# The last expert's second layer of the last chunk in seven block products

## The chip, the cores and the metric

The kernel runs on one core of a Trainium2 chip. The metric is the time of one execution in microseconds (us) on the device; smaller is better. The core has TensorE (PE, matrix products, from SBUF into the accumulators of PSUM), VectorE (DVE), ScalarE (ACT) and GpSimd (POOL) for elementwise work, and SyncE (SP), which here issues DMAs. PE, DVE, ACT, POOL and SP each work through their own list of instructions in order and wait for each other by semaphores.

## The reference

An attention with pooled keys and values makes the tokens `x`; a layer of four experts follows, and its second product is what the change is about:

```
scores = scale * (q @ mean8(k).T);  x = softmax(scores) @ mean8(v)      # B=8, H=8, S=576, D=64
x -> (4608, 512);  p = domain_probs / sum(domain_probs)
for e in range(4):
    h = max(x @ w1[e], 0)             # (4608, 1024)
    out += p[:, e] * (h @ w2[e])      # (4608, 512)
```

## The kernel before

The 4608 tokens are worked on in nine chunks `c` of 512 tokens; the ninth (`c = 8`) holds the last 64 tokens of each of the eight batches (`x_rem`). For each chunk the four experts `e` follow each other. `order` lists the 32 pairs (c, e) from chunk 1 on, and a loop over slots `g` writes down, seven slots to a pair, which instruction each engine gets next. The schedule is by hand: every engine executes its instructions in the order in which this Python text calls them.

*Seven products.* Both layers cut their two matrices into 2 x 2 quarters and make the product from seven block products of sums and differences, not eight plain ones (Winograd's form). For the second layer, `quarters` names the quarters of the hidden matrix: `a11`, `a12`, `a21`, `a22` (rows are 256 tokens, columns 512 hidden values). `hidden_sums(c, e, part)` makes the sums on DVE by `combine` (L246), each over 128 x 1024 bf16:

- part 0: `S3 = a11 - a21`
- part 1: `S2 = a22 - S3`
- part 2: `a21 = a21 + a22`, in place
- part 3: `a12 = a12 - S2`, in place

`weight_sums` makes the sums of `w2` once, into `wt_bf[:, e]` (three quarters, `t[:, 0]` to `t[:, 2]`), and writes `b22 - b12` over the quarter `b12` of `w2_bf`. So after that the plain `b12` of an expert is gone.

*`down(c, e, step)`* (L746) is one of the seven block products: 8 matmuls of 128 x 256 outputs (L763), into one of two PSUM banks, `chains[0]` and `chains[1]` (o_ps in the profile). The steps of a pair lie in consecutive slots, between steps of the first layer (`up_product`, L695) of the next pairs. After each step, `add` (L842) multiplies the result by the token's probability and adds it to `acc` in SBUF: one DVE instruction for each block of 128 tokens, two to a step. For a step in `POOLED` (here step 4) the way is another: two ACT instructions write the scaled blocks to `addend` (L775), and one POOL instruction adds `addend` to `acc` (L777).

*`up_product`* (L695) works in `units[0]` and `units[1]`, two PSUM banks each (`unit` in the profile). Its step 5 ends with a relu on ACT that writes a half of `a21` (L716); its step 6 ends with a relu on DVE that writes a half of `a22` (L675). The last `up_product` of the kernel is unit 1, step 6, of the pair (8, 3), in the last slot, `g = 224`.

*The end.* In that slot step 6 of (8, 2) follows. Then `down_last` (L809) does the second layer of (8, 3) with eight plain block products: for each half `row` of the tokens and each half `col` of the columns, two blocks of 8 matmuls (L822) into one bank of `units` (for the last quarter into two banks), 64 matmuls. After each quarter come two `add`s on DVE and one `store` (L846). Since the plain `b12` of expert 3 is gone, `load_last_weights` (L798) has read it once more into `room`, by a DMA from POOL's queue in slot 210.

*`store`* for the last chunk issues two DMAs, one on SP's queue and one on ACT's (L856), each with the 64 tokens of one batch parity. The last quarter is stored block by block, so there are five stores, ten DMAs.

Of the kernel before, what the change touches and what calls it, by code (L numbers as in the profile page):

```python
# [9 lines left out]
ACT = mybir.ActivationFunctionType  # L10
ALU = mybir.AluOpType
# [6 lines left out]
def kernel(  # L18
# [10 lines left out]
    nc = tc.nc  # L29

    B, H, S, D = q.shape
    E, DM, F = moe_w1.shape
    P = nc.NUM_PARTITIONS
# [4 lines left out]
    NR = NT // P  # L38
    REM = S - NT
    KC = DM // P  # L40
    FCH = F // P
# [15 lines left out]
    HF, HN, HD, HK = FCH // 2, NT // 2, DM // 2, KC // 2  # L57
    FH = F // 2
    LO, HI = slice(0, HF), slice(HF, FCH)
    BLOCKS = 2  # L60
# [5 lines left out]
    units = [None, None]  # L66
    chains = [psum.tile([P, NT], F32, name=f"o_ps{i}") for i in range(2)]
# [6 lines left out]
    w2_bf = wpool.tile([P, E, FCH, DM], BF16, name="w2_bf")  # L74
    wu_bf = wpool.tile([P, E, 3, HK, FH], BF16, name="wu_bf")
    wt_bf = wpool.tile([P, E, 3, HF, HD], BF16, name="wt_bf")
    acc = const.tile([P, NR, DM], F32, name="acc")
    x_rem = const.tile([P, NPAIR, NT], BF16, name="x_rem")
    ident = const.tile([P, P], BF16, name="ident")
    partial = const.tile([P, 2, 2, NT], F32, name="partial")  # L80
    addend = const.tile([P, BLOCKS, HD], F32, name="addend")
    S2 = const.tile([P, HF, HN], BF16, name="S2")
    S3 = const.tile([P, HF, HN], BF16, name="S3")
# [90 lines left out]
    def load_q(b):  # L174
        q_sb = raws[("q", b)] = qpool.tile([P, H, NR, D], BF16, name="q_sb")
        src = q[b, :, 0:NT, :].rearrange("h (p r) d -> p h (r d)", r=NR)
        if b:
            nc.gpsimd.dma_start(out=q_sb[:].rearrange("p h r d -> p h (r d)"), in_=src)
            return
        for group, queue in enumerate((nc.sync, nc.scalar)):  # L180
            hs = slice(4 * group, 4 * group + 4)
            queue.dma_start(out=wide_q[:, hs], in_=src[:, hs])
# [38 lines left out]
    p_all = const.tile([P, NBLK, E], F32, name="p_all")  # L221
# [23 lines left out]
    def combine(dst, a, op, b):  # L245
        nc.vector.tensor_tensor(out=dst, in0=a, in1=b, op=op)  # L246
# [352 lines left out]
    hidden = {(0, 0): H_bufs[0], (0, 1): H_bufs[1], (0, 2): H_third, (0, 3): H_bufs[0]}  # L599
    order = [(c, e) for c in range(1, NCH) for e in range(E)]  # L600
# [130 lines left out]
    def quarters(c, e):  # L731
        H_sb = hidden[(c, e)]
        return H_sb[:, 0, 0], H_sb[:, 1, 0], H_sb[:, 0, 1], H_sb[:, 1, 1]

    def hidden_sums(c, e, part):
        a11, a12, a21, a22 = quarters(c, e)
        if part == 0:
            combine(S3[:], a11, ALU.subtract, a21)
        elif part == 1:
            combine(S2[:], a22, ALU.subtract, S3[:])  # L740
        elif part == 2:
            combine(a21, a21, ALU.add, a22)
        else:
            combine(a12, a12, ALU.subtract, S2[:])
# [48 lines left out]
        if fcs.stop == FCH:  # L793
            add(o_ps, c, e, r, slice(0, DM), True)

    room = wu_bf[:, 0, 0].rearrange("p k (i d) -> p (k i) d", d=HD)

    def load_last_weights():  # L798

        nc.gpsimd.dma_start(  # L800
            out=room, in_=moe_w2[E - 1][0:FH, HD:DM].rearrange("(fc p) d -> p fc d", p=P)
        )

    def last_weights(fc, col):
        if col and fc < HF:
            return room[:, fc, :]
        return w2_bf[:, E - 1, fc, col * HD:(col + 1) * HD]

    def down_last(c, e):  # L809

        H_sb = hidden[(c, e)]
        banks = units[0] + units[1]
        for row in (1, 0):
            for col in range(2):
                cols = slice(col * HD, (col + 1) * HD)
                both = [banks[2 * row + col]] * BLOCKS
                if not row and col:
                    both[1] = chains[0]
                ps = [ps[:, j * HD:(j + 1) * HD] for j, ps in enumerate(both)]
                for j in range(BLOCKS):  # L820
                    for fc in range(FCH):
                        nc.tensor.matmul(  # L822
                            ps[j], lhsT=H_sb[:, fc // HF, row, fc % HF, j * P:(j + 1) * P],
                            rhs=last_weights(fc, col),
                            start=(fc == 0 and (j == 0 or both[1] is not both[0])),
                            stop=(fc == FCH - 1), skip_group_check=True,
                        )
                for j in range(BLOCKS):
                    add(ps[j], c, e, row * BLOCKS + j, cols, False)
                    if not row and col:  # L830
                        store(c, row, cols, j)
                if row or not col:
                    store(c, row, cols)

    def add(o_ps, c, e, r, cols, first):

        prob = p_all[:, c * NR + r, e:e + 1]
        dst = acc[:, r, cols]
        if e == 0 and first:
            nc.scalar.activation(out=dst, in_=o_ps, func=ACT.Copy, scale=prob)  # L840
        else:
            nc.vector.scalar_tensor_tensor(  # L842
                out=dst, in0=o_ps, scalar=prob, in1=dst, op0=ALU.mult, op1=ALU.add,
            )

    def store(c, row, cols, j=None):  # L846
        rs = slice(row * BLOCKS, (row + 1) * BLOCKS)
        if j is not None:
            rs = slice(rs.start + j, rs.start + j + 1)
        if c < B:  # L850
            rows = out[c * S:c * S + NT, :].rearrange("(p r) d -> p r d", r=NR)
            nc.sync.dma_start(out=rows[:, rs, cols], in_=acc[:, rs, cols])
        else:
            by_batch = out.rearrange("(b s) d -> s b d", s=S)[NT:S]
            for bb, queue in enumerate((nc.sync, nc.scalar)):
                queue.dma_start(  # L856
                    out=by_batch[:, 2 * rs.start + bb:2 * rs.stop:2, cols],
                    in_=acc[bb * REM:(bb + 1) * REM, rs, cols],
                )
# [172 lines left out]
    with tc.manual_schedule(  # L1032
            engines={ENG.PE, ENG.DVE, ENG.Activation, ENG.Pool, ENG.SP}):
        load_q(0)
        load_first(k, "kraw", 0)
        load_first(k, "kraw", 1)
        choose_rows()
        make_identity(nc, ident[:])
        load_first(v, "vraw", 0)
        load_first(v, "vraw", 1)  # L1040
        nc.gpsimd.memset(p_all[:], 0.0)
        load_probs()
        load_w1(0)
        load_w1(1)
        clear()
        rows_chosen(0)
        rows_chosen(1)
        load_w1(2)
        load_w2(0)
        load_w1(3)  # L1050
        attention_first()
        psum_first.__exit__(None, None, None)
        psum_last = ctx.enter_context(
            tc.tile_pool(name="psum_last", bufs=1, space=bass.MemoryType.PSUM))
        units[:] = [[psum_last.tile([P, NT], F32, name=f"unit{u}{i}") for i in range(2)] for u in range(2)]
        load_whole(1, k, "kraw")
        load_q(1)
        load_w2(1)
        load_whole(1, v, "vraw", 2)
        load_w2(2)  # L1060
        first_chunk()


        N = len(order)
        later, amid = pieces_later()
        below_of = [(0, 3)] + order
        sums = {}
        for at, pieces in (((3,), weight_sums(3)[3:]), ((10, 10, 11, 11), weight_sums(1)), ((10, 15, 22, 14), weight_sums(2))):
            for slot, piece in zip(at, pieces, strict=True):
                sums.setdefault(slot, []).append(piece)  # L1070
        POOLED = (4,)
        for g in range(7 * N + 1):
            t, i = divmod(g, 7)
            if i in (0, 2, 3) and 1 < g < 7 * N:
                hidden_sums(*below_of[t], i)
            t2, i2 = divmod(g - 1, 7)
            ups = [(*order[t], 0, i)] if t < N else []
            if 0 <= t2 < N:
                ups.append((*order[t2], 1, i2))

            for args in reversed(ups) if g in amid else ups:
                up_product(*args)
            if g in amid:
                amid[g]()
            if i == 1 and 1 < g < 7 * N:
                hidden_sums(*below_of[t], i)
            if g == 0:

                down_plain(0, 2, NR - 1)
            else:  # L1090
                down(*below_of[t2], i2, t2 % 2, POOLED)
            for piece in later.get(g, ()):
                piece()
            for piece in sums.get(g, ()):
                piece()
            if g == 7 * (N - 2):
                load_last_weights()
        down_last(*order[-1])
# [1 line left out]
_INS = ['q', 'k', 'v', 'moe_domain_probs', 'moe_w1', 'moe_w2']  # L1100
_OUTS = [((4608, 512), 'float32')]
# [25 lines left out]
```

## Time and profile before

| what | value |
|---|---|
| median of 3 runs (lowest, highest) | 489.56 us (489.51, 490.53) |
| profiled execution, and its span from the first to the last instruction | 489.93 us, 488.2 us |
| PE busy, share of the span | 480.5 us, 98% |
| DVE busy | 376.9 us, 77% |
| ACT busy | 303.8 us, 62% |
| POOL busy | 119.4 us, 24% |
| `down_last`, 64 matmuls, first start to last end | 476.77 to 483.92 us |
| the ten DMA issues of the last chunk, first start to last end | 479.68 to 485.30 us |

All times in the text are counted from the start of the span. The profile is one execution, 0.37 us above the median. A busy PE is not a PE at its peak, since the records of matmuls overlap: one 128 x 256 matmul has a record of 0.27 us, while the next begins 0.109 us after it. In a line of the timeline stand the start, the duration, the engine, the line of the code, the operation with its output and inputs, and how many instructions were merged; in brackets, the idle time of the engine ahead of it and what ended that. "SPq" and "ACTq" are the issues of DMAs by these queues.

### The profile page before, as it was taken

How to read it: one execution, taken by the hardware profiler on the slowest of the kernel's cores; microseconds unless marked ns; L12 is line 12 of the kernel's file. 1: busy time of each engine (PE TensorE's matmuls, PEld its weight loads, DVE VectorE, ACT ScalarE, POOL GpSimd, SP SyncE). 2: the span in 40 equal slices, each digit the busy share in tenths (PEclk: the TensorE clock that was granted, in tenths of full speed). 3: DMA queues.
4: the chain of work that ended last, by engine and by line, in shares of the span. 5: the costliest groups of instructions: out<-in, count | busy, mean ns of one | idle time of the engine just before them, and what ended most of it. 6: DMA issues, size and time to landing. Idle time of an engine off the chain costs nothing.

```text
span 488.2 us, 11522 instructions
## 1 busy us (share of the span) xinstructions
PE 480.5 (98%) x4673; PEld 409.4 (84%) x4678; DVE 376.9 (77%) x758; ACT 303.8 (62%) x576; POOL 119.4 (24%) x120
## 2 busy tenths in 40 slices
PE   8999999999999999999999999999999999999996
PEld 4669568898888888888888888888898888888885
DVE  4779799989768976798679866997678766876674
ACT  5677446855676567656765567556755567556650
POOL 8520504242523154016321442111011101010000
PEclk9999999999999999999999999999999999999999
DMA  9999999994986489345954298311111010004003
GB/s 195 203 209 203 204 170 155 103 90 54 110 110 63 77 86 137 35 83 56 159 50 91 27 165 66 68 23 66 35 23 23 23 64 3 12 23 87 1 1 87
DMA packets 104996, 41.96 MB, mean 86 GB/s; under 512 B 75504, under 2 KB 104432, under 8 KB 104944
## 3 DMA queue, kind: packets, MB, share of 16 engines
q0 software_dynamic: 58496, 22.35, 41.8%
q1 hardware_dynamic: 45328, 17.84, 16.7%
q10 hardware_dynamic: 1120, 1.05, 0.6%
q8 instruction: 36, 0.59, 0.5%
q14 instruction: 16, 0.13, 0.1%
HBM read 45.69 MB, written 9.44 MB: 113 GB/s over the span
## 4 chain that ended last, share of the span: by engine, by line
PE 91%; DMA 3%; ACT 2%; DVE 2%; POOL 1%; issue 1%; POOLq 0%; ACTq 0%
PE unit L695 42%; PE o_ps L763 41%; DMA w_bf<-in_moe_w_dram 3%; PE att L467 1%; PE unit L822 1%; PE o_ps L617 1%; PE att L393 1%; ACT expT L549 1%; PE unit L617 1%; PE unit L393 0%; DVE wt_bf L246 0%; POOL wt_bf L142 0%; ACT qT L378 0%; DVE acc L842 0%; PE work_first L631 0%
## 5 line engine op out<-in xcount | busy, mean ns | idle before, releaser
L842 DVE SCALAR_TENSOR_TENSOR acc<-o_ps,p_all,acc 128x256 f32<-128x256 f32 (+1 forms) x285 | 126.9, 485 | 52.9 <-PE o_ps L763 36.5
L763 PEld LDWEIGHTS <-H 128*128 128x128 bf16 x1320 | 129.1, 98 | 15.5 <-issue 0.6
L695 PEld LDWEIGHTS <-w_bf 128*128 128x128 bf16 x1088 | 105.2, 98 | 13.0 <-issue 0.2
L675 DVE CUSTOM_DVE_ANT_0 H<-unit,partial 128x512 bf16<-128x512 f32 x128 | 87.2, 684 | 23.8 <-ACT partial L710 11.5
L763 PE MATMUL o_ps<-w_bf,H 128*128 128x256 bf16 x792 | 102.6, 273 | 0.4 <-ACT o_ps L771 0.4
L695 PE MATMUL unit<-xT,w_bf 128*128 128x256 bf16 x704 | 100.5, 273 | 0.0
L777 POOL TENSOR_TENSOR acc<-acc,addend 128x512 f32<-128x512 f32 x24 | 30.7, 1279 | 253.2 <-ACT addend L775 202.2
L710 ACT COPY partial<-unit 128x512 f32<-128x512 f32 x128 | 72.3, 592 | 30.2 <-PE unit L695 30.2
L695 PEld LDWEIGHTS <-wu_bf 128*128 128x128 bf16 x816 | 77.6, 98 | 11.7 <-issue 2.5
L695 PE MATMUL unit<-xs,wu_bf 128*128 128x256 bf16 x512 | 77.0, 273 | 0.0
L763 PE MATMUL o_ps<-wt_bf,H 128*128 128x256 bf16 x528 | 68.4, 273 | 0.0
L712 ACT ACTIVATE H<-unit 128x512 bf16<-128x512 f32 x66 | 39.8, 605 | 30.9 <-PE unit L695 30.9
L763 PEld LDWEIGHTS <-S 128*128 128x128 bf16 x528 | 51.7, 98 | 6.0
L716 ACT ACTIVATE H<-unit 128x512 bf16<-128x512 f32 x66 | 39.6, 602 | 25.6 <-PE unit L695 25.3
L708 ACT COPY unit<-unit 128x512 f32<-128x512 f32 x68 | 39.4, 582 | 23.6 <-PE unit L695 18.0
L695 PE MATMUL unit<-xs,w_bf 128*128 128x256 bf16 x256 | 38.4, 273 | 0.0
L840 ACT ACTIVATE acc<-o_ps,p_all 128x256 f32<-128x256 f32 x72 | 30.7, 485 | 9.4 <-PE o_ps L763 7.7
L152 POOL DMA_DIRECT2D kraw<-in_k_dram x20 | 26.3, 1317 | 39.0 <-DMA kraw<-in_k_dram 39.0
L695 PE MATMUL unit<-xT,wu_bf 128*128 128x256 bf16 x240 | 35.7, 272 | 0.0
L763 PE MATMUL o_ps<-w_bf,S 128*128 128x256 bf16 x264 | 34.2, 273 | 0.0
L763 PE MATMUL o_ps<-wt_bf,S 128*128 128x256 bf16 x264 | 34.2, 273 | 0.0
L152 POOL DMA_DIRECT2D vraw<-in_v_dram x20 | 28.4, 1420 | 18.8 <-DMA vraw<-in_v_dram 18.5
(162 smaller groups left out, 500.2 us busy)
## 6 DMA issues: line engine op xcount, KB each, us to landing
out_dram<-acc SPq DMA_DIRECT2D x32, 256.0 KB, 4.2
w_bf<-in_moe_w_dram POOLq DMA_DIRECT2D x10, 512.0 KB, 17.4
q_sb<-in_q_dram POOLq DMA_DIRECT2D x7, 512.0 KB, 9.6
vraw<-in_v_dram POOLq DMA_DIRECT2D x22, 144.0 KB, 6.5
kraw<-in_k_dram POOLq DMA_DIRECT2D x21, 144.0 KB, 5.7
w_bf<-in_moe_w_dram POOLq DMA_DIRECT2D x2, 1024.0 KB, 17.8
w_bf<-in_moe_w_dram POOLq DMA_DIRECT2D x4, 256.0 KB, 7.3
wt_bf<-in_k_dram POOLq DMA_DIRECT2D x4, 144.0 KB, 5.4
```

Of the source, the lines that this page charges most:

```text
L152: nc.gpsimd.dma_start(out=raw[:], in_=rows_of(src, b, 2 * part, 2 * part + 2), accum_op=ALU.add if part else ALU.bypass)
L617: nc.tensor.matmul(out_ps, lhsT=w1_bf[:, e, kc, fc * P:(fc + 1) * P], rhs=xT[:, kc, at], start=(kc == 0), stop=(kc == KC - 1), skip_group_ ...
L675: nc.vector._custom_dve(TENSOR_ADD_SAT, out=dst, in0=ps, in1=part, s0=LARGEST, s1=0.0)
L695: nc.tensor.matmul(ps[:, n * HN:(n + 1) * HN], lhsT=lhs[:, kc, f:f + P], rhs=rhs[:, kc, :], start=(not grows and n == 0 and kc == 0), stop ...
L708: nc.scalar.copy(out=banks[1][:], in_=ps)
L710: nc.scalar.copy(out=part[:, step - 2], in_=ps)
L712: nc.scalar.activation(out=quarter(0, 0), in_=ps, func=ACT.Relu)
L716: nc.scalar.activation(out=quarter(0, 1), in_=ps, func=ACT.Relu)
L763: nc.tensor.matmul(ps[:, j], lhsT=lhs[:, i, j * P:(j + 1) * P], rhs=rhs[:, i, :], start=(not grows and i == 0 and j == 0), stop=(i == HF - 1),
L777: nc.gpsimd.tensor_add(out=dst, in0=dst, in1=addend[:])
L840: nc.scalar.activation(out=dst, in_=o_ps, func=ACT.Copy, scale=prob)
L842: nc.vector.scalar_tensor_tensor(out=dst, in0=o_ps, scalar=prob, in1=dst, op0=ALU.mult, op1=ALU.add,)
```

## The change

`down_last` now makes the second layer of (8, 3) from seven block products, 56 matmuls. The sums grow in two banks for the token blocks, `X` (`units[0]`) and `Y` (`units[1]`), and in one bank for both blocks, `third` (the other of `chains`). The order on PE is: `a11` into X; then step 6 of (8, 2), which has been taken out of the slot loop and now goes the way of `POOLED` (ACT, then POOL); then `a21 + a22` into `third`, `S2` into X, `a12` into Y, `S3` into X, `less` into `third`, `a22` into X. Here `less` is `a12 - S2`, written to the quarter `a11` of the pair before. ACT copies the two blocks of X to Y after the first product. The first contents of `third` go by ACT to `spare` (a part of `partial`) and by POOL to `acc`; after each later product DVE has two adds. The five stores follow the adds: row 0 left, row 1 right, row 0 right, and row 1 left by blocks. The sums `S3` and, after it, `a21 + a22`, `S2` and `less` are new on DVE for this pair; `S3` is called ahead of the last `up_product`. `load_last_weights` is gone.

```diff
-    def load_last_weights():
...
-    def down_last(c, e):
...
+    def down_last(c, e, flip):
+
+        w, t = w2_bf[:, e], wt_bf[:, e]
+        a11, a12, a21, a22 = quarters(c, e)
+        less = hidden[(c, e - 1)][:, 0, 0]
+        X, Y = units
+        third = [chains[1 - flip][:, j * HD:(j + 1) * HD] for j in range(BLOCKS)]
...
+        def product(banks, lhs, rhs, grows):
+            for j in range(BLOCKS):
+                for i in range(HF):
+                    nc.tensor.matmul(
+                        banks[j][:, 0:HD], lhsT=lhs[:, i, j * P:(j + 1) * P], rhs=rhs[:, i, :],
+                        start=(not grows and i == 0 and (j == 0 or banks is not third)),
+                        stop=(i == HF - 1), skip_group_check=True,
+                    )
+
+        def add_both(banks, row, cols, room=None, stored=True, split=False):
+            if room is not None:
                 for j in range(BLOCKS):
...
+                    prob = p_all[:, c * NR + row * BLOCKS + j, e:e + 1]
+                    nc.scalar.activation(out=room[:, j], in_=banks[j][:, 0:HD], func=ACT.Copy, scale=prob)
+                dst = acc[:, row * BLOCKS:(row + 1) * BLOCKS, cols]
+                nc.gpsimd.tensor_add(out=dst, in0=dst, in1=room)
+            else:
                 for j in range(BLOCKS):
...
+                    add(banks[j][:, 0:HD], c, e, row * BLOCKS + j, cols, False)
+                    if split:
                         store(c, row, cols, j)
...
+            if stored and not split:
+                store(c, row, cols)
+
+        product(X, a11, w[:, LO, left], False)
+        for j in range(BLOCKS):
+            nc.scalar.copy(out=Y[j][:, 0:HD], in_=X[j][:, 0:HD])
+        hidden_sums(c, e, 2)
+        hidden_sums(c, e, 1)
+        combine(less, a12, ALU.subtract, S2[:])
+        down(c, e - 1, 6, flip, (6,))
+        product(third, a21, t[:, 0], False)
+        add_both(third, 1, right, spare, stored=False)
+        product(X, S2, t[:, 1], True)
+        add_both(X, 0, right, stored=False)
+        product(Y, a12, w[:, HI, left], True)
+        add_both(Y, 0, left)
+        product(X, S3, w[:, LO, right], True)
+        add_both(X, 1, right)
+        product(third, less, w[:, HI, right], True)
+        add_both(third, 0, right)
+        product(X, a22, t[:, 2], True)
+        add_both(X, 1, left, split=True)
...
+            if g == 7 * N:
+                hidden_sums(*order[-1], 0)
...
-            else:
+            elif g < 7 * N:
                 down(*below_of[t2], i2, t2 % 2, POOLED)
...
-            if g == 7 * (N - 2):
-                load_last_weights()
-        down_last(*order[-1])
+        down_last(*order[-1], (N - 1) % 2)
```

More of the change, by code (lines that the diff above doesn't have):

```diff
@@ L794, in down_plain @@
             add(o_ps, c, e, r, slice(0, DM), True)
-    room = wu_bf[:, 0, 0].rearrange("p k (i d) -> p (k i) d", d=HD)
-    def load_last_weights():
[L800 to L807, printed above, removed]
-    def down_last(c, e):
[L811 to L819, printed above, removed]
-                for j in range(BLOCKS):
[L821 to L827, printed above, removed]
@@ new lines, in down_last @@
+    def down_last(c, e, flip):
[4 more added lines that the diff above has]
+        third = [chains[1 - flip][:, j * HD:(j + 1) * HD] for j in range(BLOCKS)]
+        left, right = slice(0, HD), slice(HD, DM)
+        spare = partial[:].rearrange("p u a t -> p (u a t)")[:, 0:BLOCKS * HD].rearrange(
+            "p (j d) -> p j d", j=BLOCKS)
+        def product(banks, lhs, rhs, grows):
[8 more added lines that the diff above has]
+            if room is not None:
+                for j in range(BLOCKS):
+                    prob = p_all[:, c * NR + row * BLOCKS + j, e:e + 1]
[3 more added lines that the diff above has]
+            else:
@@ L828, in down_last @@
                 for j in range(BLOCKS):
-                    add(ps[j], c, e, row * BLOCKS + j, cols, False)
-                    if not row and col:
+                    add(banks[j][:, 0:HD], c, e, row * BLOCKS + j, cols, False)
+                    if split:
                         store(c, row, cols, j)
-                if row or not col:
-                    store(c, row, cols)
+            if stored and not split:
+                store(c, row, cols)
+        product(X, a11, w[:, LO, left], False)
```

## The prediction

> **What bounds the kernel now.** I read the page first, for its chain of work that ended last:
>
> ```profile
> PE 91%; DMA 3%; ACT 2%; DVE 2%; POOL 1%; issue 1%; POOLq 0%; ACTq 0%
> ```
>
> TensorE (PE) carries nine tenths of the way to the end, so work taken from it can shorten the run, but only in the few microseconds that the change touches. So I read the same chain in order of time, for the last part (start, duration, what, how many):
>
> ```profile
> 476.06 0.87 PE o_ps L763 x8
> 476.93 6.11 PE unit L822 x56
> 483.05 0.89 PE o_ps L822 x8
> 483.93 0.02 issue
> 483.96 0.48 DVE acc L842
> ```
>
> The 64 matmuls of `down_last` (L822) stand end to end: 6.98 us from 476.93 to 483.92, 0.109 us each. Nothing makes PE wait; then comes one add of VectorE (DVE). Next the timeline before them (start, duration, engine, line, operation), for what PE, DVE, ScalarE (ACT) and GpSimd (POOL) do when the last hidden values arrive:
>
> ```profile
> 474.79 0.60 ACT L716 ACTIVATE H<-unit 128x512 bf16<-128x512 f32 x1
> 475.46 0.60 PE L695 MATMUL unit<-xs,w_bf 128*128 128x256 bf16 x4
> 475.66 0.88 DVE L842 SCALAR_TENSOR_TENSOR acc<-o_ps,p_all,acc 128x256 f32<-128x256 f32 x2 [0.62 <-PE o_ps L763]
> 475.90 1.04 PE L763 MATMUL o_ps<-wt_bf,H 128*128 128x256 bf16 x8
> 476.45 0.68 DVE L675 CUSTOM_DVE_ANT_0 H<-unit,partial 128x512 bf16<-128x512 f32 x1
> ```
>
> The plain products multiply what ACT and DVE wrote, with nothing between. Seven products need sums of those values, and the relu at 476.45, the last of them, ends at 477.13. Last, the stores, from narrow windows of the timeline:
>
> ```profile
> 483.12 0.60 SPq L856 DMA_DIRECT2D out_dram<-acc  x1
> 483.12 0.63 ACTq L856 DMA_DIRECT2D out_dram<-acc  x1
> 483.79 0.86 ACTq L856 DMA_DIRECT2D out_dram<-acc  x1
> 484.47 0.54 SPq L856 DMA_DIRECT2D out_dram<-acc  x1
> 484.75 0.55 ACTq L856 DMA_DIRECT2D out_dram<-acc  x1
> ```
>
> The last add ends at 484.44, but ACT's queue is still issuing the store before, so its half of the last store goes out at 484.75. The span ends 3.48 us after that (landing, then the closing steps). So three issues in a row on one queue already set the end: the third-last store counts as much as the last.
>
> **What goes off the path at no cost.** The reload of 512 KB (L800) issues at 439.5 in 0.84 us of POOL's queue and lands 5.9 us later, 30 us before its reader; POOL is 24% busy. Removing it gives nothing.
>
> **PE.** Eight matmuls fewer: 8 x 0.109 = 0.87 us less. The first of the seven products takes the slots from 475.90 (its `a11` is long written, its banks were emptied at 475.04); step 6 of expert 2 moves behind it, 476.77 to 477.64. The next product reads `a21` after the sum `a21+a22`. On DVE that sum is queued so: the two adds at 475.66, the new sum `S3` in the slot of 476.45, the relu 0.60 later at 477.05, ending at 477.73, then `a21+a22`, which waits for the relu's result. What a wait between two DVE operations costs is in these rows:
>
> ```profile
> 464.23 0.68 DVE L246 TENSOR_TENSOR S<-H 128x1024 bf16<-128x1024 bf16 x1
> 464.83 0.68 DVE L675 CUSTOM_DVE_ANT_0 H<-unit,partial 128x512 bf16<-128x512 f32 x1
> ...
> 23.57 0.69 DVE L246 TENSOR_TENSOR S<-H 128x1024 bf16<-128x1024 bf16 x1
> 24.36 0.69 DVE L246 TENSOR_TENSOR S<-H,S 128x1024 bf16<-128x1024 bf16 x1
> ```
>
> Independent, the second starts 0.60 after the first, before the first has ended; dependent, 0.10 after its end. So `a21+a22` runs 477.83 to 478.51. The Trainium skill (VectorE: DVE Perf Modes, The DRAIN you can't avoid) says that a semaphore after each operation costs nothing extra; by that rule the sum would start 0.19 earlier and my total be +0.8. These rows show 0.79 against 0.60, and I go by them.
>
> PE's weight load starts 0.05 after such a result (13.82 to 13.87 at L455), so at 478.56. Whether the load's own 98 ns then adds is not shown (bounds 0 and 0.10; I take 0.10, since here nothing covers it). PE restarts at 478.66 instead of 477.64: a stall of 1.02 us, at least 0.92. It eats the 0.87 saved: the last matmul ends near 484.06, 0.14 later than 483.92.
>
> Later sums do not stop PE: `S2` ends at 479.11 and is read at 479.53; `S4` (into `less`) ends at 479.89 and is read at 482.15.
>
> **The adds.** From 478.66 the products take 0.87 us each: `third` 478.66, X 479.53, Y 480.41, X 481.28, `third` 482.15, X 483.03 to 483.90. Each is followed by two DVE adds, 0.40 apart back to back and 0.48 to the end: 0.80 against 0.87, so DVE keeps up. With 0.04 from a matmul's end to an add, and block ends 0.60 and 1.04 after a product's start, the adds start at 480.17 and 480.61, 481.05 and 481.49, 482.03 and 482.43, 483.23 and 483.63, 484.03 and 484.42. Each X product finds its bank read 0.4 us or more before. `third` is one bank for both blocks, so its adds wait for the whole product (483.19), and the last two adds queue behind them: the last ends at 484.90, 0.46 later than now.
>
> **ACT and POOL.** New: two copies X to Y, four scaled copies, two POOL adds. The pair of scaled copies at 473.97 (L775) took 0.84, POOL's add behind it (L777) 1.27, starting 0.13 after the pair's end. The second copy must wait for the relu (477.73), the scaled pair of step 6 ends near 478.97, its POOL add at 480.37; the pair of `third` ends at 480.57, its POOL add at 481.97. The add on row 1, right half, waits for it: 482.03 instead of 481.92, swallowed with 0.4 to spare. Cost nothing; uncovered from 0.4 late on.
>
> **The stores.** They leave at 482.0, 482.9, 484.14 (`third`), 484.54 and 484.93, against 479.68, 481.47, 483.12, 483.79 and 484.47 now. On ACT's queue from 484.14: 0.63, gap 0.04, 0.86, gap 0.10, and the last issue starts at 485.77, where it starts at 484.75 now: +1.02. If the 0.86 was a chance and the issue takes the 0.55 of its neighbour: +0.71. SP's (0.6 and 0.56) stays ahead of ACT's.
>
> Sum: +1.0 us. Bounds: +0.6 with both low ends, +1.2 if the relu behind `S3` takes 0.79 too where I took 0.60. The profiled execution of 489.93 (span 488.2, 1.7 around it) becomes 490.9; it was 0.37 above the median of 489.56, so the median becomes 490.6. A measurement of this kernel can tell about 0.2%, here 0.98 us: the sum lies on that edge.
>
> **Rivals.**
> - *The stores come too close* (18%). All of them now start after 482.0. In the window from 484.0 to 486.6 this trace moves 0.52 MB at a mean of 202 GB/s. If 1.05 MB ran at that rate from 483.2 (1.2 us after the first issue), the last byte would go at 488.4 instead of 486.5: +1.9, 491.5. Against it: slices of that window reach 300 GB/s, which would need 3.5 us and hide behind the issues. The Trainium skill (DMA: Bandwidth & Descriptors, Issuing engines are not separate DMA queues) says that DMAs of both queues run on the same 16 engines and interleave; that speaks for this rival.
> - *The issues get shorter* (14%). The end is the queue of issues; with 0.55 each after `third`, the last starts 0.5 to 0.7 later than now: 490.1 to 490.3, not slower by what can be told. It decides if ACT's issue of the fourth store takes under 0.8. For it: nine of ten issues take 0.54 to 0.73. Against: it is the same place in the same sequence.
> - *Adds fall behind PE* (9%). If the POOL adds or the scaled copies are over 0.4 late, the adds of row 1 hold the X bank and PE waits again: each 0.5 late is 0.5 at the end, +1.5 to +2, up to 491.6. POOL's 24 adds at 1.26 to 1.58 speak against it.
> - *Faster by over 0.2%* (4%). Even without any stall, `third` would be stored at 483.2, no earlier than the third-last store now, so the queue of issues would give back the 0.87. It would take the stall gone and shorter issues both. The sum would have to be ready at 477.59, and DVE's last adds before it cannot start before 475.66.
>
> **The numbers.** The sum as worked has 55%; its own range is +0.8 to +1.2, and 32 of the 55 fall above 0.98, since small waits that I did not price only add. Slower: 32 + 18 + 9 = 59%; same: 23 + 14 = 37%; faster 4%. The range goes from just under the shorter issues, 489.9, to the adds' 491.6.
>
> **What would show it.** PE should idle 0.9 to 1.0 us ahead of the first `third` product, released by DVE's L246, and nowhere else after it; its last matmul should end near 484.0. The adds should end near 484.9, and the third-last store should issue near 484.1. A PE gap ahead of an X product would mean the adds' rival; a longer way from the last issue to its landing, the stores'. A span under 488.2 would prove the order of steps wrong.

## The result and the profile after

The changed kernel takes 490.97 us (median of 9 runs, 490.77 to 492.64), the kernel before 489.89 us (median of 9, 489.44 to 490.53). The ratio is 1.0028, with a 95% interval of 1.0018 to 1.0038. The forecast was +1.0 us; the medians differ by 1.08 us, the ratio says 0.9 to 1.9 (its middle is 1.4).

The profiled execution has a span of 489.0 us, only 0.8 above the one before. But it came to the end of the common part 0.30 us sooner. That point lies anywhere from 474.8 to 477.0 us in the profiles of this case, so these 0.30 us of one pair of profiles say nothing about the change. So from here on times are also counted from A, the start of the last first-layer product's matmuls (475.46 before, 475.16 after). From A to the end of the span it is 12.77 us before and 13.87 after: +1.10, in line with the medians.

The chain that ended last, in order of time (start, duration, what, how many), of the changed kernel:

```profile
475.34 0.02 issue
475.36 0.88 DVE acc L858 x2
476.24 0.60 DVE S L246
476.84 0.60 DVE H L675
477.44 0.61 DVE H L246
478.05 0.05 issue
478.09 1.05 PE o_ps L810 x8
479.14 2.62 PE unit L810 x24
481.76 0.89 PE o_ps L810 x8
482.65 0.02 issue
482.67 1.27 DVE acc L858 x3
```

Before, the matmuls of `down_last` stood in this chain end to end. Now the chain leaves PE at 475.34, runs through five DVE operations in a row (two adds, `S3`, the relu and `a21 + a22`), and comes back to PE at 478.09. PE's own list was free at 477.34, so it stood 0.75 us. After that its six products follow each other without a gap, 0.87 us each, and the chain ends in DVE's adds. The last matmul ends 8.35 us after A, where it ended 8.46 after A before: 0.87 saved, 0.75 given back.

The stores of the changed kernel, from narrow windows of the timeline (start, duration, queue):

```profile
481.44 0.74 ACTq L872 DMA_DIRECT2D out_dram<-acc  x1
482.71 0.63 ACTq L872 DMA_DIRECT2D out_dram<-acc  x1
483.58 0.71 ACTq L872 DMA_DIRECT2D out_dram<-acc  x1
484.33 0.80 ACTq L872 DMA_DIRECT2D out_dram<-acc  x1
485.23 0.55 ACTq L872 DMA_DIRECT2D out_dram<-acc  x1
```

The last issue starts 10.06 after A (9.29 before), and the last DMA lands 12.29 after A (11.47 before). So the end loses 0.82 us by the landing, although PE was done 0.11 sooner. What is left of the 1.10, 0.29 us, comes after the landing, in the closing steps (below).

What the DMA engines moved shows the rest. The row of GB/s in 40 slices of 0.25 us, from 3 us after A on, of the kernel before:

```profile
GB/s 0 0 0 0 0 0 0 0 0 0 147 188 160 344 201 41 0 168 184 201 344 152 0 66 209 156 271 348 312 303 250 176 8 0 0 0 0 0 0 0
```

and of the changed kernel:

```profile
GB/s 0 0 0 0 0 0 0 0 0 0 0 0 0 0 0 0 0 0 102 201 152 279 311 143 234 246 271 340 266 213 311 307 275 308 254 17 0 0 0 0
```

Before, there are pauses between the stores. After, 1.05 MB leave in one piece, from 7.5 to 11.9 us after A, some 240 GB/s.

### The profile page after: what moved, and what is told of

The parts are those of the page before. It is cut to its first block, busy times and chain, and to the rows that moved or that the text cites. A ratio compares the mean times of both kernels' runs of the same rounds, so it can differ in the third digit from the quotient of the medians.

```text
span 489.0 us, 11529 instructions
## 1 busy us (share of the span) xinstructions
PE 480.2 (98%) x4670; PEld 408.6 (84%) x4670; DVE 378.9 (77%) x762; ACT 305.9 (63%) x582; POOL 121.6 (25%) x121
## 3 DMA queue, kind: packets, MB, share of 16 engines
q10 hardware_dynamic: 1120, 1.05, 0.6%
## 4 chain that ended last, share of the span: by engine, by line
PE 91%; DMA 3%; DVE 3%; ACT 1%; POOL 1%; issue 1%; DVEq 0%; POOLq 0%; ACTq 0%
PE unit L695 42%; PE o_ps L763 41%; DMA w_bf<-in_moe_w_dram 3%; PE att L467 1%; PE o_ps L617 1%; PE att L393 1%; DVE acc L858 1%; PE unit L617 1%; PE unit L810 1%; PE unit L393 0%; DVE wt_bf L246 0%; POOL wt_bf L142 0%; PE o_ps L810 0%; ACT qT L378 0%; PE work_first L631 0%
## 5 line engine op out<-in xcount | busy, mean ns | idle before, releaser
L777 POOL TENSOR_TENSOR acc<-acc,addend 128x512 f32<-128x512 f32 x25 | 32.5, 1300 | 256.3 <-ACT addend L775 204.6
```

Of the source, the lines that this page charges most:

```text
L777: nc.gpsimd.tensor_add(out=dst, in0=dst, in1=addend[:])
```

## The experiments

All times after A, in us; the ratio is to the kernel before, with its 95% interval.

| kernel | ratio | PE ends | last add ends | last issue | last landing | end |
|---|---|---|---|---|---|---|
| before | 1 | 8.46 | 8.98 | 9.29 | 11.47 | 12.77 |
| changed | 1.0028 (1.0018 to 1.0038) | 8.35 | 9.17 | 10.06 | 12.29 | 13.87 |
| e1 no sums | 1.0011 (1.0002 to 1.0021) | 7.59 | 8.41 | 9.29 | 11.56 | 13.14 |
| e2 one last store | 1.0017 (1.0008 to 1.0026) | 8.35 | 9.17 | 9.20 | 12.20 | 13.59 |
| e3 before, one last store | 0.9993 (0.9983 to 1.0003) | 8.46 | 8.98 | 9.02 | 11.81 | 12.86 |
| e4 sum ahead | 1.0034 (1.0021 to 1.0046) | 8.38 | 9.26 | 10.16 | 12.46 | 14.05 |
| e5 step 6 on DVE | 1.0030 (1.0018 to 1.0042) | 8.35 | 9.17 | 10.04 | 12.44 | 13.73 |
| e6 before, 5 memsets | 1.0004 (0.9995 to 1.0013) | 8.46 | 8.98 | 9.29 | 11.47 | 12.77 |
| e7 without block 0 | 1.0013 (1.0004 to 1.0023) | 8.35 | 9.17 | 9.20 | 11.89 | 13.26 |
| e8 other order | 1.0029 (1.0019 to 1.0039) | 8.81 | 9.63 | 10.50 | 12.89 | 14.49 |
| e9 before, 6 memsets | 1.0001 (0.9991 to 1.0012) | 8.46 | 8.98 | 9.29 | 11.46 | 13.08 |
| e10 half a store | 1.0026 (1.0017 to 1.0036) | 8.35 | 9.17 | 10.07 | 12.06 | 13.64 |
| e11 one store more | 1.0037 (1.0024 to 1.0051) | 8.35 | 9.17 | 10.93 | 12.98 | 14.45 |

The intervals are 0.1% wide to either side, 0.5 us. The traces tell smaller things, though each is one execution: the kernel before, e6 and e9, which differ only by memsets long before the end, agree within 0.01 us up to the landing.

**e1: the sums taken out.**

```diff
-        hidden_sums(c, e, 2)
-        hidden_sums(c, e, 1)
-        combine(less, a12, ALU.subtract, S2[:])
...
-            if g == 7 * N:
-                hidden_sums(*order[-1], 0)
```

> Leaves out the four sums of the last pair (S3, a21 + a22, S2, less), so the products of the end read what lies there; all else is as in the changed kernel. Theory (PE stands 0.75 us for VectorE's queue ahead of the first product into third): the gap ahead of it goes, and the end comes 0.7 to 0.8 us earlier than in the changed kernel, some 0.3 above the kernel before, because the queue of store issues gives back the rest. Rival (the adds and the stores alone set the end, the PE gap is covered): under 0.2 us earlier than the changed kernel. Rival (GpSimd's chain decides): the add on row 1, right half, still starts at the end of GpSimd's second add, and less than 0.4 us is won.

PE's gap is gone (it ends at 7.59, 0.87 before the kernel before) and the landing is 0.73 earlier, as the theory said. But with the whole saving on PE the last issue is at 9.29, the very place of the kernel before, and the landing at 11.56 is 0.09 behind it. The third-last store is where they meet: it goes out at 7.66 in both, because in both PE has done the same 56 matmuls behind the first layer when its result is complete. The eight that are saved would have come behind it. In the changed kernel the stall of 0.75 lies ahead of it and moves it to 8.42. So the stall is what separates the changed kernel's landing from the one before; and with these five stores the 0.87 saved on PE does not reach the end, stall or not.

**e2, e7, e10, e11: what sets the end behind the adds.**

```diff
-        add_both(X, 1, left, split=True)
+        add_both(X, 1, left)
```

> The changed kernel with its last quarter stored as one pair of DMAs in place of two pairs. Theory (three issues in a row on ScalarE's queue set the end): the last issue starts near 484.4 in place of 485.2; its DMA is twice as large, which gives back 0.2 to 0.4; the end comes 0.4 to 0.7 us earlier. Rival (the transfers bind): the last landing stays where it is, within 0.2 us.

The last issue came 0.86 earlier, the landing 0.09, the end 0.28 (the rest lies in the closing steps). The theory's 0.4 to 0.7 failed; the rival's 0.2 at the landing held. The larger DMA alone does not explain it: in e3 one of that size lands 2.8 us after its issue, here 3.0.

```diff
-                    if split:
+                    if split and j:
                         store(c, row, cols, j)
```

> The changed kernel without the fourth store (the first block of the last quarter is left out of the output). Theory (the issues in a row set the end): the last issue starts near 484.36 in place of 485.2 and lands 2.2 us later, 0.8 us earlier than in the changed kernel. Rival (the transfers bind): the last landing moves by what 128 KB take at 300 GB/s, 0.4 us, or less.

The issue again 0.86 earlier, the landing 0.40, as the rival had it. Against e2, with the last issue at the same place (9.20), 128 KB less land 0.30 earlier: the transfers.

```diff
-        add_both(third, 0, right)
+        add_both(third, 0, right, stored=False)
+        store(c, 0, slice(HD, HD + HD // 2))
```

> The changed kernel with the third-last store (row 0, right) writing half of its columns; the other half is left out of the output. As many issues, 128 KB less. Theory of the prediction (issues in a row set the end): the last issue near 10.06 us and the last landing near 12.29 us after the start of the last first-layer product, as in the changed kernel, within 0.1. Rival, which the runs with one issue less now speak for (the transfers of all five stores run without a break and set the end): the last landing is 0.3 to 0.4 earlier although the last issue stays.

With all issues in place (the last at 10.07) and 128 KB less, the landing is 0.23 earlier. A queue of issues alone would have left it where it was; transfers alone would have given 0.3 to 0.4, if their time goes by bytes; the number of DMA packets (1185) stayed. The last landing comes 1.99 after its issue here, 2.23 in the changed kernel.

```diff
-        add_both(third, 0, right)
+        add_both(third, 0, right, split=True)
```

> The changed kernel with the third-last store cut into two, one for each block: one pair of issues more, the same bytes, and half of them 0.4 us earlier. Theory of the prediction: the last issue on ScalarE's queue is 0.3 to 0.5 later, and the last landing as much later. Rival (the transfers set the end): the last landing stays within 0.15 of the changed kernel's or comes earlier, as long as the last issue is less than 0.5 later.

One pair of issues more, the same bytes: the last issue was 0.87 later, not 0.3 to 0.5, and the landing 0.69 later. The slices of this run, from 3 us after A, show the DMA engines running dry:

```profile
GB/s 0 0 0 0 0 0 0 0 0 0 0 0 0 0 0 0 0 0 106 201 156 283 283 180 225 238 254 283 340 258 262 230 144 0 188 242 148 193 17 0
```

So both limits are there, and in the changed kernel they lie within some 0.3 us of each other. With fewer issues the bytes bind (e2, e7); with fewer bytes the landing comes 0.23 us earlier and then, it seems, the issues bind (e10); with more issues the issues bind (e11). The Trainium skill (DMA: Bandwidth & Descriptors, Issuing engines are not separate DMA queues) has one half of this: DMAs that several engines issue run on the same 16 DMA engines. The same section of the Trainium skill calls the time of an issue usually small beside the DMA. It is not small here: 0.55 to 0.80 us for each issue of the changed kernel on ACT's queue, against 2.2 from the last issue to its landing, and five issues on that queue.

**e3: the last store in one on the kernel before.**

```diff
-                    if not row and col:
-                        store(c, row, cols, j)
-                if row or not col:
-                    store(c, row, cols)
+                store(c, row, cols)
```

> The kernel before with its last quarter computed in one go and stored as one pair of DMAs; the quarter then lies in one bank, so both adds wait for its last matmul. Theory: the last add ends 0.4 later, the last issue starts near 484.9 in place of 484.75, and the larger DMA adds 0.2 to 0.4: 0.3 to 0.6 us slower than the kernel before. If the split did nothing there: within 0.2 us.

The expectation misdescribed the edit: the last quarter still lay in two banks, so the first block's add was not held up, and the last issue came at 9.02, not later. The landing is 0.34 later, because the DMA twice as large took 2.8 us from its issue in place of 2.2. The time is the same within the interval. So splitting the last store gains a third of a microsecond at the landing there, and 0.25 of it is lost in the closing steps: from landing to end it is 1.04 in e3 and 1.29 before. With one pair of stores less they are shorter in e2 and e7 too (1.40 and 1.37 in place of 1.58), but in e11, with one pair more, they also are (1.46). What they depend on is not shown.

**e4: the sum that PE waits for called ahead of the relu.**

```diff
                 hidden_sums(*order[-1], 0)
+                hidden_sums(*order[-1], 2)
...
-        hidden_sums(c, e, 2)
         hidden_sums(c, e, 1)
```

> The changed kernel with a21 + a22 called ahead of the last relu. Theory: the gap ahead of the first product into third falls from 0.75 to some 0.15 us and one of 0.3 opens ahead of the next, for S2; but the relu is 0.6 later, so is ScalarE's copy to Y, and behind it the scaled copies and both adds of GpSimd; the add on row 1, right half, starts near 482.0 to 482.4, the last X product waits for it, and the end is where it was or up to 0.4 us later. Rival (only PE's gaps count): 0.3 us earlier than the changed kernel.

PE's part of the timeline (first and second product after the gap, and the last one):

```profile
479.09 1.05 PE L810 MATMUL o_ps<-wt_bf,H 128*128 128x256 bf16 x8
480.29 1.05 PE L810 MATMUL unit<-wt_bf,S 128*128 128x256 bf16 x8 [0.15 <-DVE S L246]
...
483.98 1.03 PE L810 MATMUL unit<-wt_bf,H 128*128 128x256 bf16 x8
```

As the theory had it: the first gap falls to 0.28 us, another of 0.33 opens ahead of `S2` (the line shows less, since the records of matmuls overlap), and the last X product waits 0.2 for the adds of row 1, which wait for GpSimd. PE ends at 8.38 against 8.35. So this move shifted the stall and did not shorten it: 0.28, 0.33 and 0.2 in place of 0.75. It is no limit of the kernel, though. In the changed kernel's trace `a22` is written by 473.53 (step 4) and `a21` by 475.08 (step 5), both ahead of the two adds that start at 475.36; calling `a21 + a22` ahead of these adds, or ahead of `S3`, was not tried.

**e5: GpSimd relieved.**

```diff
-        down(c, e - 1, 6, flip, (6,))
+        down(c, e - 1, 6, flip)
```

> The changed kernel with the two adds of step 6 of expert 2 on VectorE, as they were, so that GpSimd has one add less. Theory: PE's gap and the last issue stay (within 0.1 us), since VectorE's two more adds are absorbed by the 0.07 that each product leaves it and GpSimd's chain was not the last; GpSimd's closing instruction, which stands 0.3 us longer in the changed kernel than in the kernel before, comes at once again if that is a matter of how many instructions GpSimd has; then 0.3 us earlier than the changed kernel. Rival (GpSimd's chain decides): the last X product starts 0.3 or more earlier.

PE ends at 8.35 and the last issue is at 10.04, both unmoved: GpSimd's chain did not decide. The first of the five stores went 0.3 us later (6.59 in place of 6.28), and the landing is 0.15 later with the last issue unmoved, as it would be if the transfers bind. The closing steps are 0.29 shorter, as the theory of GpSimd's list had it.

**e6 and e9: five and six memsets on GpSimd, in the kernel before** (the edit of e9; e6 has `range(5)`).

```diff
                 load_last_weights()
+                for _ in range(6):
+                    nc.gpsimd.memset(tiny[:], 0.0)
```

> The kernel before with five memsets of 128 x 1 on GpSimd behind the reload, where GpSimd is idle, so that it has as many instructions as in the changed kernel. Theory (the length of GpSimd's list sets the closing gap): the gap ahead of its last instruction grows from 0.06 to some 0.35 us and the end comes 0.3 later. Rival (the gap belongs to the late adds or to the stores): no change.

> The kernel before with six memsets of 128 x 1 on GpSimd in place of five, which should bring GpSimd's list to the length of the changed kernel's (197 records; the run with five has 196). Theory (the length of the list decides, at one exact place): the gap ahead of GpSimd's last instruction grows from 0.06 to 0.35 us, the end comes 0.3 later. Rival: it stays at 0.06, and the gap belongs to something else in the changed kernel.

With five nothing changed; with six, the end moved from 12.77 to 13.08 while the landing stayed (11.46). GpSimd then has 197 records in the trace, as many as in the changed kernel. The median of e9 (489.97 us, as the kernel before beside it) cannot show 0.3 us: its interval reaches to 0.6 above.

**e8: another order of the products.**

```diff
-        hidden_sums(c, e, 2)
+        hidden_sums(c, e, 0)
         hidden_sums(c, e, 1)
+        hidden_sums(c, e, 2)
         combine(less, a12, ALU.subtract, S2[:])
         down(c, e - 1, 6, flip, (6,))
-        product(third, a21, t[:, 0], False)
-        add_both(third, 1, right, spare, stored=False)
+        product(Y, a12, w[:, HI, left], True)
+        add_both(Y, 0, left, spare)
         product(X, S2, t[:, 1], True)
         add_both(X, 0, right, stored=False)
-        product(Y, a12, w[:, HI, left], True)
-        add_both(Y, 0, left)
+        product(third, a21, t[:, 0], False)
+        add_both(third, 1, right, stored=False)
```

> The seven products in another order: a11 into X, step 6 of expert 2, a12 into Y (its first contents and this go to acc by ScalarE and GpSimd), S2 into X, a21 + a22 into third (added by VectorE), S3 into X, less into third, a22 into X; the relu goes ahead of the new sums. Theory: no gap ahead of the third product, since the relu and the copy to Y end by 477.3, S2 by 478.2 and the sum by 478.8; one gap of 0.2 to 0.3 ahead of less, which waits until third is read; PE ends 0.5 earlier than in the changed kernel, the last issue is 0.5 to 0.6 earlier, still no earlier than in the kernel before. Rival: VectorE falls behind and the gaps only move: less than 0.2 earlier.

The first half held: no gap ahead of the third product, and the next ones follow without one. Then it failed. VectorE fell behind, as the rival had it, but by a cause that neither had: DVE's sum `less` took 1.76 us in place of 0.69, beside an add of GpSimd that had begun 0.16 earlier (more on this pair in the last section):

```profile
479.21 1.37 POOL L777 TENSOR_TENSOR acc<-acc,addend 128x512 f32<-128x512 f32 x1 [2.61 <-ACT addend L775]
...
479.37 1.76 DVE L246 TENSOR_TENSOR H<-H,S 128x1024 bf16<-128x1024 bf16 x1
```

DVE's adds came late, PE stood 0.91 us for them ahead of the X product of `S3` and 0.3 more ahead of the product of `less`, and the end is 0.6 later than in the changed kernel. No version with seven products beats the kernel before.

## Why the prediction was right, and where it was wrong

Its sign and its size (+1.0 against +1.08 by the medians) came out, and so did the path: a stall ahead of the first `third` product, none behind it, then the queue of stores. Slower by over 0.2% had 59%: the ratio of 1.0028 lies there, though its interval just reaches below. But two terms were off by nearly the same amount in opposite ways, so the close total flatters it.

- **Eight matmuls less, 0.87 us:** as said. **The reload at no cost:** nothing in these runs contradicts it; it was not tried alone.
- **The stall, 1.02 us:** measured 0.75. The failed step is "then `a21+a22`, which waits for the relu's result". The text before the prediction says that step 6 writes a half of `a22`; in the code it writes a half of `a12`, and `a22` is written by step 4. So the sum waits for nothing but DVE's order and starts 0.60 after the start of the relu, not 0.10 after its end (rows below the list). That is 0.18 of the error. The other 0.09 is the weight load: PE starts 0.06 after the sum's end, and the first product after the gap takes 0.88 us to the next one in place of 0.87, so of the 0.10 put in for the load some 0.01 to 0.02 is there.
- **What a wait between two DVE operations costs:** `less` starts 0.04 after the end of `S2`, on which it depends, so 0.72 from start to start, against 0.60 for independent ones. The rule of the Trainium skill (VectorE: DVE Perf Modes, The DRAIN you can't avoid) that the semaphore costs nothing extra does not carry over to these pairs, but my 0.79 was the dearer of the two values in the traces.
- **The adds:** the last one ended 0.19 later than before, where 0.46 was said; the difference is the stall's 0.27. Their order and the queueing behind `third` were as written.
- **ACT and POOL, "0.4 to spare":** covered, as e5 shows, but GpSimd's add of step 6 took 1.77 us in place of 1.27, the second had to wait for it, and the add on row 1 waited 0.34 for that. Some 0.12 us were left: the second add on row 1 starts at 482.15, may be followed 0.40 later, and is followed 0.52 later.
- **"Three issues in a row on one queue already set the end":** half right. The last issue moved by 0.78 (1.02 less the stall's 0.27 would be 0.75), and the landing by 0.82; and e1 bears out what the prediction says under its 4%, that without a stall the queue of issues gives the 0.87 back. But e2 and e7 show that the transfers alone would have ended nearly there too. The rival of the stores, given 18%, had a mechanism that is there and too high a price: 202 GB/s where the trace shows 240.
- **Closing steps:** taken as unchanged, they cost 0.29 more. That this cancels the stall's 0.27 is luck. Without the longer steps the total would have been +0.8; with them and the stall as I had sized it, some +1.4, outside the sum's own bounds.

The rows of the changed kernel for the second and third point: the relu, `a21 + a22`, `S2` and `less`.

```profile
476.75 0.68 DVE L675 CUSTOM_DVE_ANT_0 H<-unit,partial 128x512 bf16<-128x512 f32 x1
477.36 0.68 DVE L246 TENSOR_TENSOR H<-H 128x1024 bf16<-128x1024 bf16 x1
477.95 0.68 DVE L246 TENSOR_TENSOR S<-H,S 128x1024 bf16<-128x1024 bf16 x1
478.67 0.69 DVE L246 TENSOR_TENSOR H<-H,S 128x1024 bf16<-128x1024 bf16 x1
```

## What to carry to other kernels

At the end of a kernel, count what must leave after the last result, not only what must be computed: here 1 MB in five stores took 4.4 us of transfer and ten issues, and a shorter computation whose results come bunched ends no earlier. Sums that a cheaper product needs are a chain on another engine; ask when its inputs exist, and which quarter each instruction writes, before counting matmuls saved. When a total comes out right, check its terms, since errors of opposite sign hide in it.

## What the runs showed of the hardware

**DVE's sums and GpSimd's adds shut each other out.** In the changed kernel the sum began first, and GpSimd's add was stretched from 1.27 to 1.77 us; in e1, without the sums, the same add takes 1.27:

```profile
478.67 0.69 DVE L246 TENSOR_TENSOR H<-H,S 128x1024 bf16<-128x1024 bf16 x1
478.71 1.77 POOL L777 TENSOR_TENSOR acc<-acc,addend 128x512 f32<-128x512 f32 x1 [2.81 <-ACT addend L775]
...
480.40 1.27 POOL L777 TENSOR_TENSOR acc<-acc,addend 128x512 f32<-128x512 f32 x1 [2.61 <-ACT addend L775]
```

In e8 the add began first, and the sum took 1.76 in place of 0.69, to 0.55 after the add's end. The Trainium skill (SBUF — State Buffer, Who interferes with whom) says that a VectorE instruction with two inputs in SBUF contends with a GpSimd instruction that reads SBUF, and that the one that issues first blocks the other; both traces agree with that. The profile of before has one such pair that overlaps by more than 0.1 us, far from the end, with the sum of two halves of `v`. It is the 1.58 in the prediction's "1.26 to 1.58", so the price stood in a row that was read as harmless:

```profile
221.50 1.58 POOL L777 TENSOR_TENSOR acc<-acc,addend 128x512 f32<-128x512 f32 x1 [11.77 <-ACT addend L775]
221.54 0.41 DVE L342 TENSOR_TENSOR vp<-vraw 72x512 bf16<-72x512 bf16 x1
```

Here the add's record began 0.04 ahead of the sum's, and yet the add was the one stretched; in e8 the add was 0.16 ahead, and the sum was. So the order of two records this close does not tell who wins. What does come back is the time after the sum: in the changed kernel, in this pair and for both late adds of e8, GpSimd's add ends 1.12 to 1.13 us after the end of the DVE sum that it met.

**A closing step depends on the length of GpSimd's list.** GpSimd's last instructions after its clearing of semaphores, before (duration, first and last start) and after:

```profile
L1122 POOLq EVENT_SEMAPHORE  x4: 17/17/17, 487.5 to 488.1; - x4
L1122 POOLq EVENT_SEMAPHORE_RANGE_CLEAR  x1: 139/139/139, 487.8 to 487.8; - x1
```

```profile
L1138 POOLq EVENT_SEMAPHORE  x4: 17/17/17, 488.0 to 488.9; - x4
L1138 POOLq EVENT_SEMAPHORE_RANGE_CLEAR  x1: 139/139/139, 488.3 to 488.3; - x1
```

From the clearing to the last of the four it is 0.3 us before and 0.6 after. In all nine kernels with 197 or more GpSimd records, the 197th comes 0.33 to 0.38 us behind the record before it. In the changed kernel, e1, e2, e4, e7, e10, e11 and e9 it is the last of the four; in e8, which has 198, it is the last but one, and the last follows it after 0.07. In the kernels with fewer, 192 (before and e3), 193 (e5) and 196 (e6), the last one comes after 0.06. Between e6 and e9 only one memset differs. So it is the place in the list that costs the 0.3 us, at least among these, and not a certain step; why was not tried.
